# The first chunk's gap rows by products and a copy instead of a transfer, and a new order at the front

## The chip, the cores and the metric

The kernel runs on one core of a Trainium2 chip. The metric is device time in microseconds: 639.92 is the median of three runs (639.26 to 641.25). The engines are named as in the profile: PE (TensorE, the matmuls; PEld its weight loads), DVE (VectorE), ACT (ScalarE), POOL (GpSimd) and SP (SyncE, which here only issues transfers). Each runs its own list of instructions strictly in order and waits on semaphores of the others.

## The reference

A gated linear attention ("gateloop") over 4 sequences, 8 heads, 768 tokens and head size 48, and behind it a feed-forward network with a squared ReLU (384 to 2048 to 384):

```python
mag = np.sqrt(a_re * a_re + a_im * a_im)
scale = np.minimum(mag, 0.999) / (mag + 1e-06)
a_re_n, a_im_n = (a_re * scale, a_im * scale)
for t in range(S):
    ar, ai = (a_re_n[:, :, t, :, None], a_im_n[:, :, t, :, None])
    new_re = ar * S_re - ai * S_im
    new_im = ar * S_im + ai * S_re
    kv = np.einsum('bhd,bhe->bhde', k[:, :, t], v[:, :, t])
    S_re, S_im = (new_re + kv, new_im)
    y[:, :, t] = np.einsum('bhd,bhde->bhe', q[:, :, t], S_re)
...
x = np.ascontiguousarray(attn_out.transpose(0, 2, 1, 3)).reshape(B * S, H * D)
h = np.maximum(x @ w_in, 0.0)
return (h * h @ w_out).astype(np.float32)
```

The weights arrive as 64-bit floating-point words and are made into 32-bit numbers on the chip.

## The kernel before, in words

The work is cut into 12 groups of two chunks; a chunk is 128 tokens of one sequence with all eight heads. Two heads lie on the 128 partitions at a time, 48 rows each, so that 32 partitions are left over. Three pairs of heads stand in three column blocks (NG = 3); the rows of the fourth pair are dealt out over the 32 free partitions of the three blocks: these are the gap rows. The attention's result x of a chunk comes out of PE with four pairs in four blocks. `tokens` (token a.7 or b.7, line 1094) copies it from PSUM to the tile x on ACT with three copies, and `fill_gaps` (token g, line 1152) then moves the fourth block into the gap rows of the other three with two transfers on SP's queue. Only then can the first product of the feed-forward network (`first_product`, token F, lines 1160 and 1176) read the chunk's x. `squared_relu` (H, lines 1166 and 1167, or 1183 and 1184) takes the product out of PSUM, and the second product (T, line 1196; Z, line 1266) follows.

For a chunk the operands are prepared in 35 steps (`make_operands`, tokens o, or p and q where a group is split into its chunks: the first two groups). They are squares and inverses on ACT and DVE (lines 834 to 896), a product scan over blocks of 8 tokens on DVE (the pairs `pr` and `ab` at line 499), the keys' scan (line 912), and products that give queries and keys (`qk`, line 499). For the first group the fourth pair's rows of queries and keys are moved out of the gap rows on PE: `heads_moved` (line 985) multiplies by a matrix of zeros and ones, `to_heads`, into a PSUM buffer of the pool `ph`, and `moved_heads` (line 990) copies the result to the tile `last` on ACT. Then the ten steps of `chunk` (tokens a and b) follow: scores (line 1045), keys turned, the mask (a product on DVE at line 499, tile a), sums over values (line 1082), x (line 1094), and the state (lines 1107, 1113, 499).

Beside this the weights come in: 16 blocks by transfer into a ring of three buffers `words` (f and j, lines 748 and 752), each with two passes on ACT (U and S, lines 677 and 685) and one on DVE (A, line 693). A first product of one chunk needs two of the first eight blocks.

The matrix `to_heads` is made on POOL from the identity (`turn_mask`, token M11, lines 596 to 603); a set of zeros is written on DVE under other M tokens (line 619). While PE would have nothing else, `keep_busy` (I, line 579) runs products of the identity whose result nobody reads. PE's products of one chunk share two PSUM buffers (`ph`).

The order of all of this is written out by hand: the string FRONT (line 1300) is a list of tokens, one for each step, and the program follows it from left to right; each token appends its instructions to the lists of the engines. Nothing reorders them afterwards.

Of the kernel before, what the change touches and what calls it, by code (L numbers as in the profile page):

```python
# [21 lines left out]
F32 = mybir.dt.float32  # L22
# [11 lines left out]
P = 128  # L34
# [395 lines left out]
def quotient_path(ctx, tc, feat, vtok, w_in, w_out, w1, w2, out, n_seq, count):  # L430
# [149 lines left out]
    to_heads = ffn.tile([P, DM], F32, name="o")  # L580
    good = const.tile([P, 1], F32, name="good")
# [6 lines left out]
    def turn_mask(step):  # L588
# [7 lines left out]
        if step == 11:  # L596
            for t in (to_heads,):
                nc.gpsimd.memset(t, 0.0)
            for hh in range(HH):
                heads = to_heads[:, 0:D].rearrange("p (r g) -> p g r", g=NG)  # L600
                heads = bass.AP(tensor=heads.tensor, offset=heads.offset + rows(hh).start,
                                ap=[heads.ap[0], [P + 1, NG], [NG, PAD]])
                nc.gpsimd.tensor_copy(
                    out=heads, in_=ident[:, pads(hh)].unsqueeze(1).to_broadcast([P, NG, PAD]))
            return
# [6 lines left out]
        if step > 1:  # L612

            for t in {2: [begun], 3: [t[:, :, :, :, C:W] for t in qk_of],
                      4: [t[:, :, 0:2, C] for t in last], 5: [t[:, at:at + PAD] for t in vt for at in (0, PAD + DM + DM // 2)] + prod,
                      6: [],
# [536 lines left out]

    def first_product_of(i, two, b):

        ps = h_ps[i, two, b] = ph.tile([P, 4, C], F32, tag="h", name="h_ps")
        for j in range(4):
            k, at = divmod((4 * two + j) * P, BLK)
            for g in range(NG):
                nc.tensor.matmul(ps[:, j], lhsT=w1_blocks[:, k, g, at:at + P],  # L1160
                                 rhs=x_of[i][:, g, b * C:(b + 1) * C], start=(g == 0),
                                 stop=(g == NG - 1))
# [107 lines left out]
    def outputs(i, r):  # L1270
# [249 lines left out]
```

## Time and profile before

| | us |
|---|---|
| median of the runs | 639.92 |
| the profiled execution's own time | 640.72 |
| its span in the trace | 639.0 |
| PE busy, warm-up products included | 622.8 |
| DVE busy | 484.4 |
| ACT busy | 431.5 |
| first first-product of the feed-forward network starts at | 43.73 |

Times in the profile count from the start of the span. "Busy" of PE holds the warm-up products too. Idle time in square brackets is the time that the engine sat idle just before the row, and what ended it by the trace's inference: a wait for several semaphores is put down to what came last among the recorded events, so that a transfer's landing can hide behind another engine's name.

### The profile page before, as it was taken

Reading aid. Unit: us, or ns where it says so; the run is one execution under the profiler, and the core shown is the slowest. Engines: PE = TensorE matmul, PEld = TensorE weight load, DVE = VectorE, ACT = ScalarE, POOL = GpSimd, SP = SyncE. Lnnn points to the kernel's source line nnn. Section 1 sums busy time; section 2 is a strip of 40 time slices with the busy share of each in tenths; the row PEclk is TensorE's granted clock in tenths of the full one; section 3 lists DMA queues with packets and bytes.
Section 4 is the critical chain, followed back from the end, with each engine's and each line's share of the span. In section 5 each row is a group of like instructions: output and inputs, shape, how many; then the busy total and the mean of one; then the engine's idle time right before and its main releaser. Section 6 shows DMA issues by size and latency. Waiting matters only on the chain.

```text
span 639.0 us, 16032 instructions
## 1 busy us (share of the span) xinstructions
PE 622.8 (97%) x6555; PEld 560.4 (88%) x6555; DVE 484.4 (76%) x967; ACT 431.5 (68%) x851; POOL 57.9 (9%) x127
## 2 busy tenths in 40 slices
PE   7979999999999999999999999999999999999996
PEld 7968787777899899899899899899989989999996
DVE  6898998978999966886878958879949859763130
ACT  5879989649586477584586577587687667644430
POOL 6351131101000011000110000100100011000000
PEclk9999999999999999999999999999999999999999
DMA  8995782381621832430721820733741641231201
GB/s 179 185 200 151 209 217 38 92 128 43 110 38 33 149 69 65 103 72 29 152 51 33 138 62 24 145 67 102 151 101 52 130 126 32 63 64 52 68 14 27
DMA packets 41623, 60.15 MB, mean 94 GB/s; under 512 B 5960, under 2 KB 29960, under 8 KB 41544
## 3 DMA queue, kind: packets, MB, share of 16 engines
q1 hardware_dynamic: 39368, 55.06, 40.0%
q0 software_dynamic: 1888, 3.69, 3.1%
q8 instruction: 52, 0.85, 0.6%
q10 hardware_dynamic: 288, 0.32, 0.2%
q14 instruction: 27, 0.22, 0.1%
HBM read 48.76 MB, written 4.72 MB: 84 GB/s over the span
## 4 chain that ended last, share of the span: by engine, by line
PE 85%; DVE 5%; ACT 4%; DMA 3%; issue 1%; POOL 0%; DVEq 0%; ACTq 0%; POOLq 0%
PE h_ps L1176 32%; PE o_ps L1266 28%; PE o_ps L1196 6%; PE a_ps L1045 5%; PE h_ps L1160 4%; PE y L1028 3%; PE y L1082 3%; PE turns L1055 2%; PE turns L1107 2%; DVE ab L499 2%; DMA raw<-in_feat_dram 1%; DVE pr L499 1%; DMA words<-in_moe_w_in_dram 1%; DVE w L693 1%; ACT room L819 1%
## 5 line engine op out<-in xcount | busy, mean ns | idle before, releaser
L1176 PE MATMUL h_ps<-x,w 128*128 128x256 f32 x960 | 211.4, 379 | 0.0
L1176 PEld LDWEIGHTS h_ps<-x,w 128*128 128x128 f32 x960 | 181.4, 190 | 23.8
L1266 PE MATMUL o_ps<-w,h 128*128 128x192 f32 x640 | 109.8, 327 | 0.1
L1183 ACT ACTIVATE h<-h_ps 128x512 f32<-128x512 f32 x80 | 47.6, 595 | 86.3 <-PE h_ps L1176 86.1
L1266 PEld LDWEIGHTS o_ps<-w,h 128*128 128x128 f32 x640 | 103.9, 190 | 1.3 <-ACT o L1139 0.6
L499 DVE TENSOR_TENSOR pr<-ab 128x384 f32<-128x384 f32 (+3 forms) x196 | 70.5, 377 | 5.2 <-ACT ab L900 1.1
L1266 PE MATMUL o_ps<-w_sum,mix 128*128 128x192 f32 x320 | 55.2, 328 | 0.0
L499 DVE TENSOR_TENSOR ab<-pr 128x48 f32<-128x48 f32 (+3 forms) x210 | 50.0, 260 | 5.3
L1184 ACT ACTIVATE h<-h 128x512 f32<-128x512 f32 x80 | 50.5, 631 | 2.6
L1266 PEld LDWEIGHTS o_ps<-w_sum,mix 128*128 128x128 f32 x320 | 51.8, 190 | 0.3
L1160 PEld LDWEIGHTS h_ps<-x,w 128*128 128x128 f32 x384 | 44.2, 192 | 5.2 <-ACT qk L819 2.3
L1160 PE MATMUL h_ps<-x,w 128*128 128x128 f32 x384 | 45.2, 276 | 2.9 <-ACT qk L819 2.1
L499 DVE TENSOR_TENSOR qk<-ab,qk 128x768 f32<-128x768 f32 (+1 forms) x56 | 46.2, 846 | 1.2
L1196 PE MATMUL o_ps<-w,h 128*128 128x384 f32 x128 | 44.8, 490 | 0.5 <-DVE w L693 0.5
L568 POOL COPY vt<-vt 64x192 f32<-64x192 f32 x48 | 23.3, 484 | 229.8 <-DMA vt<-in_vtok_dram 188.8
L499 DVE TENSOR_TENSOR room<-ab,carry 128x1344 f32<-128x1344 f32 (+1 forms) x28 | 36.8, 1355 | 9.3 <-ACT carry L946 9.2
L1094 ACT COPY x<-y 64x256 f32<-64x256 f32 (+1 forms) x72 | 26.6, 370 | 21.4 <-PE y L1082 20.4
L1139 ACT ACTIVATE o<-o_ps 128x192 f32<-128x192 f32 (+1 forms) x44 | 15.1, 342 | 37.9 <-PE o_ps L1266 29.5
L819 ACT ACTIVATE ab<-raw 128x768 f32<-128x768 f32 (+1 forms) x28 | 38.5, 1381 | 0.0
L819 ACT ACTIVATE room<-z 128x768 f32<-128x768 f32 (+1 forms) x27 | 37.0, 1420 | 1.5 <-DVE z L866 1.3
L1045 PE MATMUL a_ps<-qk 48*64 48x64 f32 (+1 forms) x1152 | 36.9, 244 | 0.0
L1045 PEld LDWEIGHTS a_ps<-qk 48*64 48x64 f32 x1152 | 35.7, 133 | 1.1 <-issue 0.7
(115 smaller groups left out, 961.8 us busy)
## 6 DMA issues: line engine op xcount, KB each, us to landing
raw<-in_feat_dram SPq DMA_DIRECT2D x40, 288.0 KB
words<-in_moe_w_out_dram SPq DMA_DIRECT2D x8, 768.0 KB
again<-in_moe_w_in_dram SPq DMA_DIRECT2D x16, 384.0 KB
again<-in_moe_w_out_dram SPq DMA_DIRECT2D x16, 384.0 KB
words<-in_moe_w_in_dram SPq DMA_DIRECT2D x8, 576.0 KB
vt<-in_vtok_dram SPq DMA_DIRECT2D x48, 96.0 KB
out_dram<-o SPq DMA_DIRECT2D x23, 192.0 KB
last<-qk SPq DMA_DIRECT2D x44, 97.5 KB
```

The lines of the kernel that those rows point to most:

```text
L499: nc.vector.tensor_tensor(out=out, in0=in0, in1=in1, op=op)
L568: nc.gpsimd.tensor_copy(out=v[half_rows(h), PAD + DM:PAD + DM + DM // 2].rearrange("t (a x) -> t a x", x=HH * D), in_=pairs[half_rows(1 - ...
L819: nc.scalar.activation(out=out.rearrange("p c j n -> p c n j"), func=AF.Copy, in_=in_.rearrange("p c (n j) -> p c n j", j=L), **kwargs)
L1028: nc.tensor.matmul(ys[p_ % 2][crossed(hh, p_), p_ // 2], lhsT=states[b][1 - c_seq % 2][rows(hh), c, columns(hh, PAD + p_ * D)], rhs=operan ...
L1045: nc.tensor.matmul(to[:, :, 2] if s else to[:, :, 0:2], lhsT=operand(2 + c, p_, rows(hh))[:, half_rows(s)], rhs=q_[:, :, 1] if s else q_, ...
L1094: nc.scalar.copy(out=x_of[gi][to, odd::2, b * C:(b + 1) * C], in_=tiles["y"][odd][of, 0:NP // 2])
L1160: nc.tensor.matmul(ps[:, j], lhsT=w1_blocks[:, k, g, at:at + P], rhs=x_of[i][:, g, b * C:(b + 1) * C], start=(g == 0), stop=(g == NG - 1))
L1176: nc.tensor.matmul(ps[:, j], lhsT=w1_blocks[:, k, g, at:at + P], rhs=x_of[i][:, g], start=(g == 0), stop=(g == NG - 1))
L1183: nc.scalar.activation(out=h, in_=h_ps[i, f], func=AF.Relu, scale=of_w1)
L1184: nc.scalar.activation(out=h, in_=h, func=AF.Square)
L1196: nc.tensor.matmul(o_of[i, b], lhsT=tokens_of(i, f, b)[:, j], rhs=w2[:, k], start=(k == 0), stop=(k == NFB - 1))
L1266: nc.tensor.matmul(to, lhsT=x(k)[:, j], rhs=factor(z)[:, 2 * k + j], start=(z in (0, 1, 3) and k == j == 0), stop=(k == KH // 2 - 1 and j ...
```

## The change

The gap rows of the first chunk (group 0, chunk 0) are no longer moved by the two transfers. A new token G does it in two steps: six products on PE put into one PSUM buffer the three blocks of x as they are (by `kept`, the identity without its gap columns) with the gap rows added (by `to_gaps`, a permutation), and one copy on ACT writes them back to x. The three matrices `to_heads`, `to_gaps` and `kept` are zeroed and filled on DVE; POOL no longer does so. `kept` lies in a buffer of the tag `again`, `to_gaps` in the second buffer of the tag `o`. The other chunks still use transfers.

```diff
     to_heads = ffn.tile([P, DM], F32, name="o")
+    to_gaps = ffn.tile([P, DM], F32, name="o")
+    kept = dec.tile([P, E // 2, 2], I32, name="again").rearrange("p e w -> p (e w)")[
+        :, 0:P].bitcast(F32)
...
         if step == 11:
-            for t in (to_heads,):
-                nc.gpsimd.memset(t, 0.0)
+            nc.vector.tensor_copy(out=kept[:, PAD:ROWS + D], in_=ident[:, PAD:ROWS + D])
             for hh in range(HH):
...
-                nc.gpsimd.tensor_copy(
+                nc.vector.tensor_copy(
                     out=heads, in_=ident[:, pads(hh)].unsqueeze(1).to_broadcast([P, NG, PAD]))
+                nc.vector.tensor_copy(
+                    out=to_gaps.rearrange("p (g m) -> p g m", g=NG)[:, :, token_pads(hh)],
+                    in_=ident[:, token_rows(hh)].rearrange("p (r g) -> p g r", g=NG))
...
-                      6: [],
+                      6: [to_heads, to_gaps, kept],
...
+    gaps_of = {}
+
+    def move_gaps(i, b, step):
+        x = x_of[i][:, :, b * C:(b + 1) * C]
+        if step:
+            nc.scalar.copy(out=x[:, 0:NG], in_=gaps_of[i, b])
+            return
+        to = gaps_of[i, b] = ph.tile([P, 2, TOK], F32, tag="h", name="o_ps").rearrange(
+            "p j t -> p (j t)")[:, 0:NG * C].rearrange("p (g t) -> p g t", g=NG)
+        for g in range(NG):
+            nc.tensor.matmul(to[:, g], lhsT=kept, rhs=x[:, g], start=True, stop=False)
+            nc.tensor.matmul(to[:, g], lhsT=to_gaps[:, g * P:(g + 1) * P], rhs=x[:, NG],
+                             start=False, stop=True)
...
-        "f4 q0.15 q0.23 j4 a0.2 q0.22 l1.2.0 a0.3 V0.0 a0.5 a0.6 a0.4 U5 a0.7 q0.24 g0.0 f6 a0.8 "
...
+        "q0.25 q0.16 i1.2.0 q0.13 q0.26 q0.27 a0.6 a0.7 j6 a0.8 U5 S5 G0.0.0 G0.0.1 F0.0.0 q0.17 "
...
+        "G": move_gaps,
```

The order is new from the program's start up to about the place where the first output is stored; behind it the list is as before. Before, 98 warm-up instructions stand at the head of PE's list; now 36, then the transposition for the mask, then 66. On ACT the copy of the second chunk's queries (line 819), which followed the copies of x, now precedes them. On SP the transfers of the first chunk's gap rows are gone, and with them SP's wait for the copies of x. Three places show the rest. In the changed file the lines stand 3 to 19 further down: line 1160 is 1179 there, 985 is 990, 1107 is 1112, 1094 is 1099, 677 is 682, 685 is 690, 693 is 698, 834 is 839, 848 is 853, 892 is 897.

PE, from the first chunk's state products to the first of the feed-forward network's products, before and now (`turns` is the state's sum, `idle` the warm-up products, `h_ps` the first product):

```order
L1107 MATMUL turns<-vt_102,kt_127 48x48 x8
L1107 MATMUL turns<-vt_102,kt_128 48x48 x8
L579 MATMUL idle<-ident 128x128 x10
L1160 MATMUL h_ps<-x,w_58 128x128 x12
L579 MATMUL idle<-ident 128x128 x2
L1160 MATMUL h_ps<-x,w_58 128x128 x12
L579 MATMUL idle<-ident 128x128 x2
L985 MATMUL o_ps<-qk_117,o 128x260 x6
```

```order
L1112 MATMUL turns<-vt_102,kt_129 48x48 x8
L1112 MATMUL turns<-vt_102,kt_130 48x48 x8
L1169 MATMUL o_ps<-x,again 128x128
L1170 MATMUL o_ps<-x,o 128x128
L1169 MATMUL o_ps<-x,again 128x128
L1170 MATMUL o_ps<-x,o 128x128
L1169 MATMUL o_ps<-x,again 128x128
L1170 MATMUL o_ps<-x,o 128x128
L1179 MATMUL h_ps<-x,w_58 128x128 x24
L579 MATMUL idle<-ident 128x128 x8
L990 MATMUL o_ps<-qk_119,o 128x260 x6
```

Six products of x took the place of ten warm-up products, and the eight warm-up products now stand behind both first products. An instruction of PE shows as two records in the trace.

ACT, around the squares of the next group (`room<-raw`), before and now (`carry` and its followers end the second chunk's totals, `h` are the squared ReLUs, `part` the passes over the weights):

```order
L949 COPY qk_117<-ab 128x2x3
L950 COPY prod_121<-ab 128x2x3
L951 ACTIVATE prod_121<-ab 128x3
L1166 ACTIVATE h<-h_ps 128x512
L1167 ACTIVATE h<-h 128x512
L677 ACTIVATE part<-words 128x768
L685 ACTIVATE part<-words 128x768
L834 ACTIVATE room<-raw 128x768
L1166 ACTIVATE h<-h_ps 128x512
L1167 ACTIVATE h<-h 128x512
```

```order
L1185 ACTIVATE h<-h_ps 128x512
L1186 ACTIVATE h<-h 128x512
L951 COPY carry<-ab 128x2x3x15
L952 ACTIVATE carry<-ab 128x3x15
L954 COPY qk_119<-ab 128x2x3
L955 COPY prod_123<-ab 128x2x3
L956 ACTIVATE prod_123<-ab 128x3
L824 ACTIVATE qk_120<-raw 128x3x16x8
L1185 ACTIVATE h<-h_ps 128x512
L1186 ACTIVATE h<-h 128x512
L682 ACTIVATE part<-words 128x768
L839 ACTIVATE room<-raw 128x768
```

Both squared ReLUs now come ahead of the squares, and one weight pass that stood ahead of them comes behind. The copy back to x (line 1164) stands further up, behind two weight passes that follow the copies of x, as the tokens U5 S5 G0.0.0 G0.0.1 in the diff say.

DVE, ahead of the first chunk's mask (`a<-a_ps,mask`), before and now:

```order
L892 SCALAR_TENSOR_TENSOR room<-room 128x384
L499 TENSOR_TENSOR ab<-ab,room 128x768
L896 SCALAR_TENSOR_TENSOR room<-z,room 128x384
L693 SCALAR_TENSOR_TENSOR w_58<-words,part 128x768
L499 TENSOR_TENSOR pr<-ab 128x192
L499 TENSOR_TENSOR ab<-pr 128x2x48
L499 TENSOR_TENSOR pr<-ab 128x192
L499 TENSOR_TENSOR ab<-pr 128x2x48
L499 TENSOR_TENSOR a<-a_ps,mask 128x768
```

```order
L897 SCALAR_TENSOR_TENSOR room<-room 128x384
L499 TENSOR_TENSOR ab<-ab,room 128x768
L901 SCALAR_TENSOR_TENSOR room<-z,room 128x384
L499 TENSOR_TENSOR pr<-ab 128x192
L499 TENSOR_TENSOR ab<-pr 128x2x48
L499 TENSOR_TENSOR pr<-ab 128x192
L499 TENSOR_TENSOR ab<-pr 128x2x48
L499 TENSOR_TENSOR a<-a_ps,mask 128x768
```

One weight block's pass (w) went behind the mask. Further up, the second chunk's sum of squares (`room<-room`, line 848, now 853), which stood ahead of the first chunk's totals (15 instructions), now stands behind them.

## Rows read from the trace of the kernel before

**Rows 1.** profile page: busy time; granted clock over 40 slices of the span
```profile
PE 622.8 (97%) x6555; PEld 560.4 (88%) x6555; DVE 484.4 (76%) x967; ACT 431.5 (68%) x851; POOL 57.9 (9%) x127
...
PEclk9999999999999999999999999999999999999999
```

**Rows 2.** windows: us, each engine's busy us (instructions), PEclk, DMA share, GB/s
```profile
0.00:43.73 43.73, 34.64 (x364) 32.65 (x364) 35.88 (x119) 32.73 (x65) 19.89 (x45) 1.00 0.94 188
43.73:60.00 16.27, 15.49 (x193) 13.98 (x194) 13.62 (x22) 13.39 (x30) 4.88 (x10) 1.00 0.70 155
60.00:90.00 30.00, 28.77 (x354) 24.10 (x353) 28.18 (x68) 28.63 (x57) 5.49 (x10) 1.00 0.71 205
90.00:125.00 35.00, 35.00 (x353) 28.37 (x353) 31.34 (x55) 30.31 (x48) 6.53 (x10) 1.00 0.41 85
125.00:639.00 514.00, 508.86 (x5299) 461.27 (x5298) 375.39 (x707) 326.48 (x654) 21.15 (x52) 1.00 0.37 78
```

**Rows 3.** chain of waits, 28 to 62 us: start us, us, what
```profile
51.71 1.55 PE o_ps L985 x6
```

**Rows 4.** instructions in time, 34 to 60 us: start, us, engine, line, operation [idle]
```profile
35.41 0.95 DVE L499 TENSOR_TENSOR a<-a_ps,mask 128x768 f32<-128x768 f32 x1
...
37.37 1.16 ACT L1094 COPY x<-y 128x256 f32<-128x256 f32 x3 [0.58 <-PE y L1082]
...
38.16 1.39 SPq L1152 DMA_DIRECT2D x<-x  x2
...
38.55 0.86 ACT L819 ACTIVATE qk<-raw 128x384 f32<-128x384 f32 x1
...
43.73 2.92 PE L1160 MATMUL h_ps<-x,w 128*128 128x128 f32 x24 [2.14 <-ACT qk L819]
...
46.68 0.60 ACT L1166 ACTIVATE h<-h_ps 128x512 f32<-128x512 f32 x1 [2.30 <-PE h_ps L1160]
...
47.84 1.07 ACT L677 ACTIVATE part<-words 128x768 int16<-128x768 uint32 x1
...
48.77 1.04 ACT L685 ACTIVATE part<-words 128x768 fp8e5<-128x768 uint8 x1
...
49.68 0.82 ACT L834 ACTIVATE room<-raw 128x768 f32<-128x768 f32 x1
...
50.53 0.56 DVE L848 SCALAR_TENSOR_TENSOR room<-room 128x384 f32<-128x384 f32 x1 [1.94 <-ACT room L834]
```

**Rows 5.** instructions in time, VectorE alone, 12.7 to 36 us
```profile
12.79 0.36 DVE L499 TENSOR_TENSOR pr<-ab 128x192 f32<-128x192 f32 x1
...
19.34 0.56 DVE L848 SCALAR_TENSOR_TENSOR room<-room 128x384 f32<-128x384 f32 x1 [1.02 <-ACT room L834]
...
31.20 0.55 DVE L892 SCALAR_TENSOR_TENSOR room<-room 128x384 f32<-128x384 f32 x1
...
33.31 0.95 DVE L693 SCALAR_TENSOR_TENSOR w<-words,part 128x768 int32<-128x768 int32 x1
34.18 0.34 DVE L499 TENSOR_TENSOR pr<-ab 128x192 f32<-128x192 f32 x1
```

**Rows 6.** instructions in time, start of the program, 0 to 60 us
```profile
3.31 0.70 DVE L619 MEMSET begun<- 128x768 f32 x1
...
6.65 0.56 DVE L848 SCALAR_TENSOR_TENSOR room<-room 128x384 f32<-128x384 f32 x1 [1.95 <-ACT room L834]
...
8.28 0.41 POOL L603 COPY o<-ident 128x48 f32<-128x48 f32 x2
```

**Rows 7.** instructions in time, 75 to 135 us
```profile
76.62 1.56 PE L1196 MATMUL o_ps<-w,h 128*128 128x384 f32 x4 [0.49 <-DVE w L693]
...
79.25 0.13 PEld L1028 LDWEIGHTS y<-last,state 48*64 48x64 f32 x1 [0.18 <-DMA last<-qk]
...
89.52 0.68 PE L1160 MATMUL h_ps<-x,w 128*128 128x128 f32 x4 [0.47 <-DMA x<-x]
...
104.72 0.50 ACT L1139 ACTIVATE o<-o_ps 128x384 f32<-128x384 f32 x1 [0.70 <-PE o_ps L1196]
```

173 rows, old and new, of the table FRONT are left out of this document.

## The prediction

> **What bounds the kernel now.** I read the page first: PE is busy for 622.8 of 639.0 us and its clock is granted in full in all 40 slices [rows 1]. Such a share can hide a front in which PE computes little of use, so I cut the span by stage [rows 2]. From 125 us on PE is busy for 508.86 of 514 us: there PE alone sets the end, DVE (375) and ACT (326) have room, and whatever time PE's useful work gains before 125 us should come off the end. Before 43.73 us PE's busy time is mostly warm-up products (the 98 instructions at the head of its list), while DVE is busy for 35.9 and the 16 transfer engines for 0.94 of the time. Between 43.73 and 90 us all three engines are busy for 82 to 96%: a chain that hops between them decides. So the question is by how much that chain moves.
>
> The order in time shows its hinges [rows 4]. The first chunk's mask starts on DVE at 35.41; x is copied from 37.37 to 38.53; the transfers of the gap rows are issued from 38.16 to 39.55; the first first-product starts at 43.73. The trace writes its wait of 2.14 us to an ACT copy, but the product reads only x and weights, x was complete by 38.53 but for the gap rows, and so it is the transfer that landed there, 4.2 us after its issue. ACT then idled 2.30 us for this product, its squares for the next group came at 49.68, DVE waited 1.94 us for them (50.53), and the chain goes on through PE's second half of `heads_moved` at 51.71 [rows 3].
>
> **The change part by part.** Where instructions follow each other I count from start to start, since a row's duration overlaps its successor's.
>
> The matrices. DVE gets three more fills and five small copies at the start. By elements the fills are 7/6 of the one of 768 (0.70 us), so 0.8 us; POOL's two copies took 0.41 together, so five on DVE cost at most 1.0 [rows 6]. DVE idled 1.95 us ahead of 6.65, and the eight state fills moved behind that instruction, into the next wait. Cost nothing; without that cover 1.8 us, and below nothing is excluded, as work is only added. POOL loses the same work, but its transfers wait for buffers, not for POOL: nothing.
>
> DVE up to the mask. From 12.79 to 31.20 its instructions are the same ones in both, in another order. The second chunk's sum of squares waited 1.02 us for ACT at 19.34 [rows 5]; it now stands behind the totals and comes some 2 us later, when ACT is done. That wait goes: 1.02. Then a weight pass (33.31 to 34.18, 0.87) moves behind the mask. Sum 1.89. What is late next is PE: 66 warm-up products stand ahead of `heads_moved`. 24 records, that is 12 instructions, took 2.92 us [rows 4], 0.24 us each, so that one or two too many cost a quarter or a half. I take 1.75: the mask at 33.66. Bounds: 0.5 (fill late) to 1.89.
>
> The gap rows. The copies of x then start at 35.62 and, as before, end their share of ACT's time 1.18 later (37.37 to 38.55). Next on ACT stand two weight passes, 0.93 and 0.91 (47.84, 48.77, 49.68), and the new copy. A copy of 128 by 384 from PSUM took 0.50 [rows 7]. So the first product may start at 35.62 + 1.18 + 0.93 + 0.91 + 0.50 = 39.14 instead of 43.73. The six new products take 6 x 0.24 = 1.46 us and lie beside the two passes (1.84). Behind the copy's wait on ACT stand the following weight passes and everything else of ACT; if the passes gave no cover, the wait would cost ACT at most 1.46. On SP a wait for ACT goes, behind which two later weight blocks and the second chunk's values stood.
>
> What this is worth downstream. The two first products now run back to back: 39.14 + 2 x 2.92 = 44.98. ACT's squares come behind the second squared ReLU (46.68 to 47.84, 1.16) and one weight pass (0.93): 44.98 + 1.16 + 0.93 = 47.07 instead of 49.68, a gain of 2.61. DVE must be ready by then: before, it reached its wait at 50.53 - 1.94 = 48.59, that is 13.18 after the mask's start; with the moved pass 33.66 + 13.18 + 0.87 = 47.71, and the squares end some 0.85 after 47.07, at 47.92. So DVE's next step stands at 47.92 instead of 50.53: 2.61 again, and both engines arrive together. The new copy and the earlier ReLU pair are counted; two things come off ACT's list here, a copy of the queries that moved ahead (38.55 [rows 4]) and one weight pass, which I leave as reserve.
>
> From there to 76 us the lists hold the same work, and DVE, the fullest, carries the 2.61 along. Later the waits of PE change a little: 0.49 for a weight pass and 0.47 for the transfer of a later chunk [rows 7] may go, since one product of the feed-forward network now stands ahead of the former. Against it the scores of the second group follow directly behind their operands' transfer, where PE waited 0.18 [rows 7]; I estimate a half. Net -0.2, in a range from -1.2 to +1.0. Sum: 2.61 - 0.2 = 2.4 us off the execution's own 640.72, so 638.3; that execution lay 0.8 above the median of 639.92, so the forecast is **637.5**. The new products and two more warm-up instructions (0.5 us) lie inside the stretch before 49 us and are paid there already.
>
> **The clock.** PE idled 2.14 us ahead of 43.73 and the granted clock stayed at full speed, 2.4 GHz, in every stretch [rows 1, 2]. The Trainium skill, TensorE: Matmul & The Clock Gate, section "Why this matters for your kernels", tells to leave no long idle gap between bursts of matmuls, since PE falls to half rate. The trace of before agrees as far as it goes: no gap in it is long, and none brings the clock down.
>
> **The rivals.** *The gain is taken back before PE fills up.* Up to 43.73 us the transfer engines are busy for 0.94 of the time, so weights could land no earlier than before, and PE's wait for a weight pass (76.62) and the operands' transfer (79.25) would stay where they are [rows 2, 7]. Then only the waits that vanish between count: 0.3 to 1.5 us, so about 639.0. For it: transfers are 0.70 busy from 43.73 to 60 and 0.71 to 90, with pieces that wait for a free buffer of three. Against it: those buffers are freed by DVE's passes, which move too, and ACT's first read of a block came long after its issue.
>
> *The clock falls.* Before, ten warm-up products stood between the state's products and the first product; now six useful ones do, and then PE waits for ACT, about 0.8 us (the six, from 36.80 on, end at 38.3, the copy at 39.1), and another time ahead of the turned mask near 13 us, where the 36 warm-up products have run out. If the clock went to 1.2 GHz there, the two first products would take 11.7 instead of 5.84 and end at 50.8, the squared ReLU, weight pass and squares behind them would put DVE's step at 53.8 instead of 50.53. That is 3.2 us slower: 643. It decides once the lower level lasts longer than some 2.7 us of lost product time, which is less than half of the two products. Against it: 2.14 us of idle before did nothing [rows 4], and full clock stands in all of rows 2. The skill's rule named above would give this same 643, if such a gap counts as a long one.
>
> That the transfer stays in the way isn't one: the first product in the new order waits for ACT and for no transfer of x.
>
> **How the numbers follow.** Forecast 0.62: 637.5, its own range 636.3 (both later waits gone too, 3.6 off) to 638.5 (1.4 off). First rival 0.26: 638.6 to 639.9. Clock 0.12: 640.5 to 643. The bound of about what a measurement can tell from no change, 0.3%, is 1.92 us: faster means under 638.0. Some nine tenths of the forecast lie there, so faster 0.55; the rest of it and the first rival make no change 0.33; slower 0.12. The range reaches from 636.0 to 640.5, which leaves out most of the clock case and the outer end of the forecast.
>
> **What would show it.** In the profile after, the mask at about 33.7, the copies of x at 35.6, the first product at 39.1, the squares at 47.1, DVE's step at 47.9, `heads_moved` near 49.1 (51.71 before), and PE's wait for a weight pass near 74. DVE's idle of 1.94 ahead of the squares should shrink to a few tenths. Wrong would be: the first product early but the squares still near 49.7; an ACT wait on a weight block's landing ahead of the new copy; a granted clock below full in the stretch from 38 to 50 us; or PE busy for less than 508 of the last 514 us, which would say that PE waits later for what it gained early.

## The result, and the profile after

| | before | after |
|---|---|---|
| median of 16 runs each, us | 640.07 | 644.88 |
| lowest to highest, us | 638.86 to 644.19 | 641.0 to 647.75 |
| profiled execution's own time, us | 640.72 | 644.23 |
| its span, us | 639.0 | 642.5 |

The changed kernel takes 1.0064 times as long (95% interval 1.0042 to 1.0087): by this ratio 4.1 us slower (the medians lie 4.8 apart), where 2.4 us faster was forecast. The four longest runs after (647.1 to 647.8) are the four with the lowest mean granted clock (0.988 to 0.992), but the five at 0.998 or more, 641.0 to 644.8 with a median of 642.1, are not faster than before either.

Windows of the changed kernel, cut at its own first first-product; the columns are those of [rows 2]:

```profile
0.00:42.42 42.42, 36.17 (x367) 34.46 (x368) 36.68 (x122) 29.62 (x61) 18.62 (x42) 0.97 0.94 191
42.42:60.00 17.58, 16.16 (x167) 14.56 (x171) 12.40 (x22) 15.12 (x30) 4.79 (x10) 0.88 0.68 118
...
125.00:642.50 517.50, 512.31 (x5354) 464.76 (x5352) 377.96 (x713) 328.21 (x657) 21.03 (x52) 1.00 0.37 78
```

The last stretch is as full as before: PE is idle for 5.19 us of it (5.14 in [rows 2]). All of the loss is ahead of 125 us, and in two of the stretches the granted clock is below full, where [rows 1] had 9 in all 40 slices. Where it fell shows in finer windows (same columns):

```profile
38.00:39.00 1.00, 0.00 (x0) 0.00 (x0) 0.96 (x2) 1.00 (x2) 0.80 (x2) 1.00 1.06 149
...
40.00:40.50 0.50, 0.50 (x4) 0.50 (x4) 0.43 (x3) 0.00 (x0) 0.00 (x0) 0.50 1.02 258
...
46.00:47.00 1.00, 1.00 (x8) 1.00 (x8) 0.11 (x1) 0.00 (x0) 1.00 (x3) 0.67 1.28 212
```

PE ran nothing between 38 and 39 us; from about 39.8 to 46.7 us it ran at 1.2 GHz. The instructions in time, the answer to [rows 4] (start, us, engine, line, operation, [idle before]):

```profile
34.11 0.96 DVE L499 TENSOR_TENSOR a<-a_ps,mask 128x768 f32<-128x768 f32 x1 [0.40 <-PE a_ps L1050]
...
36.05 0.83 PE L1112 MATMUL turns<-vt,kt 128*48 128x48 f32 x26
36.07 1.14 ACT L1099 COPY x<-y 128x256 f32<-128x256 f32 x3 [0.46 <-PE y L1087]
...
39.01 0.38 PE L1112 MATMUL turns<-vt,kt 128*48 128x48 f32 x6 [2.14 <-issue]
...
39.65 0.44 PE L1170 MATMUL o_ps<-x,o 128*128 128x128 f32 x2
...
39.88 0.64 PE L1169 MATMUL o_ps<-x,again 128*128 128x128 f32 x2
...
41.89 0.48 ACT L1164 COPY x<-o_ps 128x384 f32<-128x384 f32 x1 [2.67 <-PE o_ps L1170]
...
42.42 7.64 PE L1179 MATMUL h_ps<-x,w 128*128 128x128 f32 x48 [0.62 <-ACT x L1164]
...
52.19 0.82 ACT L839 ACTIVATE room<-raw 128x768 f32<-128x768 f32 x1
...
53.04 0.56 DVE L853 SCALAR_TENSOR_TENSOR room<-room 128x384 f32<-128x384 f32 x1
```

Read it from the middle. The state's products (line 1112) are 32 records in one go; 26 run, then PE stands for 2.14 us, put down to "issue", that is to nothing that the profile shows, and then the last 6 run. The six new products stand behind them, so that ACT's copy waits 2.67 us for them. Those six run at half speed from the third one on (two records in 0.64 us after 0.44), and the two first products take 7.64 us. The squares end up at 52.19 (49.68 in [rows 4]). The chain of waits goes through the same pause:

```profile
36.88 2.14 issue
```

### The profile page after: what moved, and what is told of

The parts are those of the page before. It is cut to its first block, busy times and chain, and to the rows that moved or that the text cites. A ratio compares the mean times of both kernels' runs of the same rounds, so it can differ in the third digit from the quotient of the medians.

```text
span 642.5 us, 16051 instructions
## 1 busy us (share of the span) xinstructions
PE 627.3 (98%) x6567; PEld 565.0 (88%) x6567; DVE 486.0 (76%) x975; ACT 431.3 (67%) x852; POOL 55.0 (9%) x124
## 4 chain that ended last, share of the span: by engine, by line
PE 94%; ACT 3%; DVE 1%; issue 1%; DMA 1%; POOL 0%; SPq 0%; ACTq 0%; POOLq 0%; DVEq 0%
PE h_ps L1195 32%; PE o_ps L1285 29%; PE o_ps L1215 6%; PE a_ps L1050 5%; PE h_ps L1179 5%; PE idle L579 4%; PE y L1033 3%; PE y L1087 3%; PE turns L1060 3%; PE turns L1112 3%; PE o_ps L990 1%; ACT part L682 1%; ACT part L690 1%; DMA last<-qk 1%; ACT h L1185 0%
## 5 line engine op out<-in xcount | busy, mean ns | idle before, releaser
L1179 PE MATMUL h_ps<-x,w 128*128 128x128 f32 x384 | 47.0, 284 | 0.6 <-ACT x L1164 0.6
L499 DVE TENSOR_TENSOR a<-a_ps,mask 128x768 f32<-128x768 f32 x24 | 22.9, 954 | 19.5 <-PE a_ps L1050 19.3
```

The costliest lines, as they stand in the source:

```text
L499: nc.vector.tensor_tensor(out=out, in0=in0, in1=in1, op=op)
```

## What the pause is

The kernel before has such a pause too. PE alone, in the kernel before:

```profile
38.20 0.94 PE L579 MATMUL idle<-ident 128*128 128x128 f32 x6
39.76 0.49 PE L579 MATMUL idle<-ident 128*128 128x128 f32 x2 [0.63 <-issue]
```

These are warm-up products, which wait for no data. How many records PE had run by then is in the PE column of a window that ends inside the pause, of before (0 to 39.5) and of after (0 to 38.9):

```profile
0.00:39.50 39.50, 32.81 (x349) 30.98 (x349) 32.06 (x99) 28.51 (x60) 19.89 (x45) 1.00 0.94 186
```

```profile
0.00:38.90 38.90, 33.38 (x349) 32.02 (x349) 33.48 (x107) 28.78 (x59) 18.62 (x42) 1.00 0.93 188
```

349 in both, though the 349th is another instruction. The profile counts 52 transfers of the kind "instruction" on queue q8, 16 KB each, one per 126 records of PE. One of them lies right here; the queues of the changed kernel from 35.6 to 37.4 us (packets, MB, share of 16 engines):

```profile
q0 software_dynamic: 72, 0.23, 71.9%
q1 hardware_dynamic: 174, 0.08, 34.8%
q8 instruction: 1, 0.02, 5.3%
```

That packet's record begins at 35.74, and at 36.47 in the kernel before; PE went on 3.27 and 3.29 us later. Beside it the transfer engines are full of data. So the theory is this: PE's instructions come in blocks; one block begins behind record 349, and when PE gets there before the block has come, it stands. The kernel before reached that record at 38.86 and lost little, among warm-up products; the changed one reached it at 36.67, among useful work. The Trainium skill, Runtime: NRT & Kernel Launch, section "Instruction fetch mechanics", has the same 16 KB blocks of 256 instructions, and 126 records of two instructions each (a product and its weight load) agree with it. The same section of the Trainium skill calls the cost of a block's edge "mostly hidden"; the traces agree but for this edge, which is the only place in PE's list, in any of the twelve profiles, where PE stands for more than 0.15 us for "issue".

## The experiments

All are edits of the list FRONT. Each is set against runs of the kernel before on the same chip; an I is two warm-up instructions, four records.

**e1: 64 records fewer ahead of the pause**

```diff
-I0 I1 I2 I3 I4 I5 I6 I7 I8 I9 I10 I11 I12
...
-I105 I106 I107
```

> The changed kernel with 32 warm-up instructions fewer (26 of the 36 ahead of the mask's turn, 6 of the 66 ahead of heads_moved): 64 records fewer in PE's list, nothing else moved. Theory A (instruction supply): PE's pause of 2.14 us, 36.88 to 39.01, stands behind the 349th product record; in the kernel before, a pause of 0.63 us stands behind the 349th record too, among warm-up products that wait for nothing, and each ended 3.3 us after a 16 KB transfer of the instruction queue had begun (35.74 and 36.47). With 64 records fewer the pause leaves the added products and falls, if it comes at all, into the first products; the gap rows' products follow at about 37.2, the first product starts at about 39.8 instead of 42.42, the clock stays full from 38 to 50 us, the squares come near 47.7 instead of 52.19, and the time is 637 to 639.5. Rival B (the added products wait for their operand): the pause stays in the added products until 39.0, the clock falls as it did, 643 to 645. Rival C (the clock falls for any idle stretch ahead of the first product): no pause in the added products, but the two first products take 7 us or more and the time is 641 to 644.

Measured: 639.34 us (12 runs) against 640.75; ratio 0.9978 (0.9962 to 0.9995).

```profile
24.69 0.56 DVE L499 TENSOR_TENSOR raw<-raw,room 128x384 f32<-128x384 f32 x1 [2.34 <-issue]
...
35.77 0.96 DVE L499 TENSOR_TENSOR a<-a_ps,mask 128x768 f32<-128x768 f32 x1
...
37.71 0.93 PE L1112 MATMUL turns<-vt,kt 128*48 128x48 f32 x32
...
40.76 0.45 ACT L1164 COPY x<-o_ps 128x384 f32<-128x384 f32 x1
...
41.26 5.62 PE L1179 MATMUL h_ps<-x,w 128*128 128x128 f32 x48 [0.94 <-ACT x L1164]
```

All 32 records of line 1112 run in one go, the copy waits for nothing, and the first products take 5.62 us at full clock. An idle stretch of 0.94 us ahead of them did not bring the clock down: rival C falls, and B with it. But a second loss comes to light: the mask starts at 35.77, 2.1 us later than I had forecast, and the first product at 41.26 instead of the 39.8 that I expected. VectorE stood 2.34 us for the keys, whose growth is the row at 24.69. Its wait is put down to "issue"; that it is for a transfer shows in the landings: in each of the seven profiles in which this row waits (after, e1, e3 and e6 to e9) it starts 0.17 or 0.18 us after the last landing of one and the same transfer into `raw`.

**e2: the price of the clock in the kernel before**

```diff
-I109 I110 I111 I112 I113
```

> The kernel before without the ten warm-up products that stand between the state's products and the first product; PE is then idle from about 38.3 to 43.73. If such a stretch brings the clock down (theory), the granted clock is 0.5 in part of 40 to 50 us, the two first products take 8 to 11.7 us together instead of 5.84, and the time is 2 to 3.5 us over that of before: this is the price of the clock alone. If the clock fell in the changed kernel for another reason (rival), the granted clock stays full, the first product stays at 43.7 and the time within 0.5 us of before.

Measured: 643.06 against 640.75; ratio 1.0039 (1.0023 to 1.0054). Windows (columns as in [rows 2]):

```profile
38.00:42.00 4.00, 0.00 (x0) 0.00 (x0) 3.58 (x17) 3.98 (x7) 0.00 (x0) 0.97 1.03 160
...
47.00:48.00 1.00, 1.00 (x7) 1.00 (x7) 0.97 (x3) 0.00 (x0) 0.56 (x2) 0.50 1.05 188
```

PE was idle for 6.30 us ahead of the first product; the clock fell and stayed at 1.2 GHz until past 48 us, which cost 2.3 us of the median (1.5 to 3.5 us by the interval); the two first products took 5.00 and 2.84 us. The mechanism of my second rival is real, and its price of 3.2 us lies inside the interval.

**e3 and e4: the order alone, the products alone**

e3 is the changed kernel with the old transfer, e4 the old order with products and copy (and the matrices on DVE; its edit is shown against the order of before):

```diff
-G0.0.0 G0.0.1
+g0.0
```

```diff
-g0.0 f6 a0.8 i1.2.0 q0.6 q0.13 q0.14 I109 I110 I111 I112 I113 U4
+G0.0.0 f6 a0.8 i1.2.0 q0.6 q0.13 q0.14 I109 I110 I111 I112 I113 G0.0.1 U4
```

> The changed kernel, order and matrices as they are, with the transfer for the first chunk's gap rows in place of the six products and the copy. Theory A (the new order leaves PE without warm-up products and with its pause): x is copied from 36.07 to 37.2, the transfer lands some 4.2 us after its issue, near 41.5, PE idles from 39.4 to there, the clock falls and the first products take 7 us or more: 642 to 646, no better than the changed kernel. Rival (the products are what costs): the first product near 41.5 at full clock, both done at 47.4, 638 to 639.5.

> The order of before with the matrices on VectorE, the six products in the place of the transfer's issue and the copy ahead of ScalarE's next weight passes; the ten warm-up products stay. Theory A (the products gain what the transfer's 4.2 us cost, less PE's pause near its 349th record): x complete near 41 instead of 42.7, first product near 41.3 instead of 43.73, clock full, time 638 to 639.5. Rival (gain taken back later): first product near 41.3, but the same time as before within 0.6 us. Rival (ScalarE's list is what pays for the copy): the squares stay near 49.7 and the time is up to 1.5 us over before.

Measured: e3 647.95, ratio 1.0105 (1.0077 to 1.0133); e4 641.89, ratio 1.0016 (0.9998 to 1.0033). Instructions in time, of e3:

```profile
25.74 0.56 DVE L499 TENSOR_TENSOR raw<-raw,room 128x384 f32<-128x384 f32 x1 [3.46 <-issue]
...
40.87 1.29 SPq L1157 DMA_DIRECT2D x<-x  x2
...
49.68 8.27 PE L1179 MATMUL h_ps<-x,w 128*128 128x128 f32 x48 [7.69 <-DMA x<-x]
```

and PE's of e4:

```profile
36.86 1.00 PE L1087 MATMUL y<-a,vt 64*64 64x128 f32 x32 [1.17 <-DVE a L499]
38.24 0.49 PE L1169 MATMUL o_ps<-x,again 128*128 128x128 f32 x2 [0.38 <-ACT x L1099]
...
42.72 2.50 PE L579 MATMUL idle<-ident 128*128 128x128 f32 x20
45.06 2.84 PE L1179 MATMUL h_ps<-x,w 128*128 128x128 f32 x24
```

The order alone is the worst of all. In e3's profile, the longest of its six runs, the transfer took 7.5 us from the end of its issue (42.16) to the product, against the 4.2 of [rows 4], and it was issued late: VectorE had waited 3.46 us for the keys, and the copies of x stand at 40.06, 4.0 us behind the changed kernel's. I missed both sizes, the first product's (41.5 expected) by 8 us. In e4 the first product came later than before (45.06, not the 41.3 that all my theories had), because the warm-up products, which had been cover, now stood behind the six and ahead of it, and the six ran at half clock (0.50 from 39.5 to 42). The interval of e4 holds 1, so that it can't be told from before. Neither half of the change helps by itself, but e4 does not price the products without warm-up products between them and the first product.

**e5: e1 with the values' load later**

```diff
-v0.0
...
-V0.0
...
 i0.1.1
+v0.0
...
 j5
+V0.0
```

> The kernel of e1 (32 warm-up instructions fewer) with the load of the first chunk's values moved behind the second chunk's keys, where the kernel before has it, and the copy that swaps the values behind two more weight transfers. In e1 VectorE waited 2.34 us for the keys' transfer ahead of 24.69, and the mask started at 35.77. Theory (the values' 192 KB, issued from 6.17 to 10.6 in front of the keys, make these land late): VectorE's wait shrinks by 0.9 to 2 us, the mask starts at 33.8 to 35.0, its step on the group's squares moves with it from 49.86 to 48.2 to 49.1, and the time falls by 0.5 to 1.5 us below that of e1. Rival (the keys wait for the weights issued in front of them, not for the values): the wait stays above 1.8 us and the time within 0.4 us of e1.

Measured: 638.59 against 640.72; ratio 0.9966 (0.9956 to 0.9977); profiled span 636.3.

```profile
22.05 0.56 DVE L499 TENSOR_TENSOR raw<-raw,room 128x384 f32<-128x384 f32 x1
...
33.70 0.96 DVE L499 TENSOR_TENSOR a<-a_ps,mask 128x768 f32<-128x768 f32 x1
...
35.66 1.14 ACT L1099 COPY x<-y 128x256 f32<-128x256 f32 x3 [0.29 <-PE y L1087]
...
39.19 5.62 PE L1179 MATMUL h_ps<-x,w 128*128 128x128 f32 x48 [0.95 <-ACT x L1164]
...
46.95 0.82 ACT L839 ACTIVATE room<-raw 128x768 f32<-128x768 f32 x1
...
47.79 0.56 DVE L853 SCALAR_TENSOR_TENSOR room<-room 128x384 f32<-128x384 f32 x1
```

Here VectorE does not wait for the keys, and the kernel is the fastest of all that were run, faster than before and after. Every step stands within 0.13 us of the prediction's. The wait shrank by all of its 2.34 us, more than I expected; the median is 0.75 under e1's, inside what I gave, though the two intervals still overlap (0.9962 to 0.9977), so that the load's own worth is not shown.

**e6 and e7: the pause moved by 24 and by 8 records**

```diff
-I0 I1 I2 I3 I105 I106
```

```diff
-I0 I1
```

> The changed kernel with 12 warm-up instructions fewer, 24 records, 8 ahead of the mask's turn and 4 ahead of heads_moved. If PE's pause belongs to a place in its list, behind the 349th record, it now stands behind the 6th record of the first first-product: the added products and the six new ones run without a gap, the first product starts 5.5 us after the mask as in e1 (41.26 - 35.77), and what is left of the pause inside it is under 1.2 us; time 638.5 to 641. If only the number of warm-up products or the early clock of e1 was what helped, the pause stays among the added products and the time is 643 to 646.

> The changed kernel with 4 warm-up instructions fewer, 8 records, all ahead of the mask's turn. If the pause belongs to the 349th record, it now stands behind the second record of the six new products, and not among the added ones; it ends as late as in the changed kernel, the copy and the first product are as late, and the time is that of the changed kernel within 1 us (643.5 to 646). If taking out warm-up products helps in itself, a part of the gain of e1 shows: under 643.

Measured: e6 641.72, ratio 1.0015 (0.9998 to 1.0033); e7 644.31, ratio 1.0064 (1.0040 to 1.0088). e6:

```profile
40.89 0.94 PE L1179 MATMUL h_ps<-x,w 128*128 128x128 f32 x6 [0.95 <-ACT x L1164]
43.17 4.96 PE L1179 MATMUL h_ps<-x,w 128*128 128x128 f32 x42 [1.34 <-issue]
```

e7:

```profile
41.36 0.49 PE L1169 MATMUL o_ps<-x,again 128*128 128x128 f32 x2
...
42.46 0.49 PE L1170 MATMUL o_ps<-x,o 128*128 128x128 f32 x2 [0.61 <-issue]
```

The pause stands where the count puts it, behind the 6th record of the first first-product and behind the 2nd of the new ones, in the midst of products that had all their operands. In both PE went on 3.1 to 3.2 us after the instruction transfer had begun (40.10 and 39.27). In e6 it left 1.34 us instead of the at most 1.2 that I gave, and the time is 0.7 over my range: the transfer began late. e7's time is that of the changed kernel, but its profiled execution is not the same story: VectorE waited 3.71 us for the keys there, PE 3.83 us for VectorE, and the clock fell at that place instead.

**e8: the changed kernel with the values' load later**

> The changed kernel with only the values' load moved behind the second chunk's keys. The pause stays among the added products; if it is what binds the first product, an earlier mask gains less than 0.6 us of first product: 643.5 to 645.5. If instead the late keys are the larger part of the loss (rival), the time falls to 641 to 643.

Measured: 643.78, ratio 1.0048 (1.0024 to 1.0071). The edit is e5's without e1's. PE's pause stays, behind record 349:

```profile
39.73 0.38 PE L1112 MATMUL turns<-vt,kt 128*48 128x48 f32 x6 [2.66 <-issue]
```

VectorE still waited for the keys:

```profile
22.84 0.56 DVE L499 TENSOR_TENSOR raw<-raw,room 128x384 f32<-128x384 f32 x1 [0.79 <-DVE room L917]
```

(This row, too, starts 0.17 us after the landing.) That is more than the 0.49 us of the changed kernel's profile (at 22.58), where the values stand ahead of the keys. So the move came without a wait in e5 and with one here; what sets the keys' landing stays open. The time is where the theory had it, and its interval covers that of the changed kernel: with the pause in place, the keys can't be told from nothing.

**e9: fewer transfers while the block is due**

```diff
-l1.2.0
...
-i1.2.0
...
 F0.1.0
+l1.2.0 i1.2.0
```

> The changed kernel with the loads of the next group's features (issued from 29.69 and 30.61, some 770 KB) moved behind both first products of the first chunk. The question is why PE's block of instructions comes so late: its transfer began at 35.74, 4.4 us after PE had passed its 223rd record. Theory (it stands behind data in the transfer engines, which are busy for 0.85 to 1.1 of 29 to 38 us): with these loads gone from that stretch it begins before 34.5, PE's pause shrinks below 1 us or goes, and the first product starts by 41. The time may gain less, as the features now land some 6 us later. Rival (the hour of the transfer is set by PE's own list): it begins within 4 to 5 us of the 223rd record as before, the pause stays at 2 to 2.7 us.

(The 223rd record was passed at 32.4 in the changed kernel, not at 31.3 as the expectation has it; the delay there is 3.3 us; and the transfer engines are busy for 0.61 of 29 to 31 us.) Measured: 646.76, ratio 1.0124 (1.0086 to 1.0161): the features came too late, and VectorE waited 3.92 us for the squares. But the pause is gone: all 32 of the state's records run in one go, and the first product starts at 40.83, by 41 as expected. PE's row and windows of e9:

```profile
37.28 0.96 PE L1112 MATMUL turns<-vt,kt 128*48 128x48 f32 x32
```


```profile
31.00:33.00 2.00, 2.00 (x11) 1.53 (x10) 1.93 (x4) 1.39 (x3) 1.01 (x2) 1.00 0.45 84
33.00:35.00 2.00, 2.00 (x66) 1.63 (x66) 1.85 (x5) 1.46 (x3) 0.00 (x0) 1.00 1.12 303
35.00:38.00 3.00, 2.96 (x83) 2.50 (x75) 2.93 (x7) 2.64 (x10) 0.00 (x0) 1.00 0.09 13
```

The instruction transfer began at 34.93, 1.3 us after the 223rd record, where in the eleven other kernels, which keep these loads ahead of the first products, it took 2.1 to 5.8 us. It began when the engines, full from 33 to 35 us, fell nearly empty (0.09). That speaks for the block standing behind data in the transfer engines. It is one profile, the start missed the 34.5 that I gave, and the mask was 1.2 us later than in the changed kernel, which helps too: at the 36.88 of the changed kernel PE would still have stood, by an estimate from the 3.0 to 3.3 us below, for some 1.0 to 1.4 us. So why the block comes late is made likely here, not settled.

**e10: the matrices alone**

The kernel before with only the matrices moved to DVE.

> The kernel before, with its order and its transfer of the gap rows, but with the matrices made on VectorE (the two for the products are made too, and not used). Theory: free, VectorE's steps at 6.65 and 19.34 stay within 0.1 us, the mask at 35.4, the time within 1 us of before. Rival: VectorE is late by the 0.8 to 1.8 us of added work and the mask and the time with it.

Measured: 640.55 against 640.48; ratio 1.0005 (0.9986 to 1.0024). The steps of [rows 5] and [rows 6]:

```profile
6.42 0.56 DVE L853 SCALAR_TENSOR_TENSOR room<-room 128x384 f32<-128x384 f32 x1 [0.77 <-ACT room L839]
...
19.04 0.56 DVE L853 SCALAR_TENSOR_TENSOR room<-room 128x384 f32<-128x384 f32 x1 [1.03 <-ACT room L839]
```

The idle time ahead of 6.65 took the work, 1.95 to 0.77. Both steps are 0.2 to 0.3 us early, where I expected them within 0.1. The matrices are free, to within the 1.5 us of the interval.

## Why the prediction was wrong

| step | predicted | after | e5 |
|---|---|---|---|
| mask | 33.66 | 34.11 | 33.70 |
| copies of x | 35.62 | 36.07 | 35.66 |
| first product | 39.14 | 42.42 | 39.19 |
| squares | 47.07 | 52.19 | 46.95 |
| DVE's next step | 47.92 | 53.04 | 47.79 |

**The step that failed** is "The six new products take 6 x 0.24 = 1.46 us and lie beside the two passes (1.84)". It took for granted that PE would come to them without a stop, at full clock. From the mask to the first product I had 5.48 us; the changed kernel needs 8.31, e1 and e5, without the pause, 5.49 each. So 2.83 us are the pause and the half-speed products behind it; e6 and e7 show that it belongs to a place in PE's list. The trace of before held the hint, 0.63 us of "issue" among warm-up products that wait for nothing. I never asked what it was; warm-up products looked like slack, and they were also what stood around the edge of the block.

**The clock rival** came near the time (643 against 644.88) by luck, with another cause and other terms. I let PE idle 0.8 us for ACT and put 5.86 us more on the two products (11.7 for 5.84); in e1 and e5 PE idles 0.95 us there at full clock. In the changed kernel the clock fell behind the pause ahead of the new products. From first product to squares I had 7.93 us (e5: 7.76); after took 9.77, that is 1.84 more, on top of the 2.83. With the mask's 0.45 this makes up the 5.12 us by which the squares miss 47.07. These sizes are those of one profiled run; the runs of the changed kernel spread from 641.0 to 647.75.

**DVE up to the mask** was mis-sized from run to run: "its instructions are the same ones in both, in another order" left out that one of them, the growth of the keys, reads a transfer. It stood at 24.36 before and would stand near 22.1 now, and the keys let it start only at 22.6 to 26.0 when the values are loaded ahead of them (at 22.05 in e5 and 22.84 in e8, where they are not). The 1.75 us that I took are there in e5 (1.71); in the profiled run after 0.45 of them are missing, in e1 2.1, more than all. The first rival, a transfer that lands no earlier, was right in kind, but it bit here and not near 76 us.

**What held.** The matrices cost nothing (e10). The products and the copy do take the gap rows off the transfer, which is dearer in the new order than I knew (7.5 us in e3, 4.2 before). And the rest of the chain came out: e5's profiled span is 2.7 us under that of before, its DVE step 2.74 earlier, and by its runs it gains 2.2 us (1.5 to 2.8); 2.4 was the forecast. Nothing of that was given back before PE fills up, although a later wait grew, 0.49 in [rows 7] to 1.02 at 74.11 in e5. In the changed kernel two grew:

```profile
79.45 1.56 PE L1215 MATMUL o_ps<-w,h 128*128 128x384 f32 x4 [1.14 <-DVE w L698]
83.02 0.32 PE L1033 MATMUL y<-last,state 48*64 48x128 f32 x1 [1.18 <-DMA last<-qk]
```

Together they grew by 1.65 us (0.49 and 0.18 in [rows 7]), and two waits of before are gone, the 0.47 of [rows 7] and one of 0.26 at 65.24: net 0.9 of the 1.0 us by which 2.51 at the squares became 3.5 at the end of the span.

**Slips in the sum.** The two more warm-up instructions that the sum counts before 49 us are not there: the traces of before and after hold 232 warm-up records each, 220 and 208 of them before 49 us. And the first rival's 0.3 to 1.5 us off 639.92 gives 638.4 to 639.6, not 638.6 to 639.9. Neither bears on the miss.

## What to carry to other kernels

A wait named "issue" on an engine whose instruction needs no data is a question to be answered before the work around it is rearranged: count the records up to it, and see whether another kernel stops at the same count. Warm-up instructions are part of an engine's list like any other; put in or taken out, they shift all the edges behind them; here 64 records fewer turned 4.1 us slower into 1.4 us faster (by the ratios). When an engine's list is reordered, follow each moved instruction's transfers too: an instruction that never waited had perhaps just come late enough.

## What the runs showed of the hardware

- PE's list comes in 16 KB blocks, one per 126 records. In the seven profiles with a pause behind record 349 (before, after, e3, e6, e7, e8, e10), PE went on 3.0 to 3.3 us after the block's transfer had begun; in the five without one, PE came to record 350 3.0 to 8.9 us after it. Small products use up a block's worth in about that time (64 records of scores in 1.6 us, 32 of sums in 1.0, 32 of state in 0.9), and the transfer itself began 2.1 to 5.8 us after the record one block earlier (1.3 in e9).
- The clock held at 2.4 GHz through single idle stretches of 2.14 us (before), 2.05 us (e1) and 2.69 us (e6), and fell to 1.2 GHz within or just behind stretches of 2.56 (e10), 3.83 (e7), 5.54 (e1, at the start) and 6.30 us (e2); it also fell behind the changed kernel's 2.14, and in e4 behind waits of 1.17, 0.38 and 0.28 us between short products. One idle stretch's length does not tell whether it falls.
- The same transfer of gap rows took 4.2 us from the end of its issue to the product in one order and 7.5 in another.
